# Reordered loads, a copy on GpSimd and a shifted transpose in the first slots of a forgetting-attention kernel

## The chip, the cores and the metric

The kernel runs on one core of a Trainium2 chip. The metric is the device time of one launch in microseconds (us); lower is better. The engines are named as the profile names them: PE is TensorE, DVE is VectorE, ACT is ScalarE, POOL is GpSimd, SP is SyncE.

## The reference, cut to what matters

Eight batches of eight heads, 576 tokens, head size 64. Attention with a forget gate `f`, then a two-layer network on the rows of all heads.

```python
scores = scale * q @ k.T                       # 8 x 8 x 576 x 576
cum = cumsum(log(clip(f, 1e-4, 1)))            # along the tokens
scores = where(causal, -1e9, scores + cum[i] - cum[j])
attn = softmax(scores) ;  x = (attn @ v) as rows of 512
h = x @ w_in ;  out = (h - tanh(h)) @ w_out    # 4608 x 512 -> 2048 -> 512
```

## The kernel before

The attention is worked in 32 slots, one for each pair of neighbouring heads (`pairs`, four pairs to a batch); slot p is pair p. The first four slots (batch 0) fill the machine: all that follows mixes attention with the network's products.

**A slot** has seven score tiles (`TILES`), numbered ti 0 to 6: three of the first head, one short "tail" tile (ti 3, `LAST`) with the last 64 tokens of both heads, three of the second head. `scores` (L337) multiplies a tile on PE into a PSUM bank, and ACT takes the exponential (L361) into a tile `e`; the tail tile goes to one of three kept tiles `EL[0..2]`, by pair number modulo 3. The banks are two of the pool `ps_sc` in turn, and in batch 0 every third tile uses the bank `ps_tr`; a bank is free for PE again once its exponential has been taken.

**Operands.** q and k of a pair are loaded with a cast by POOL's DMA queue (`load_qk`), turned by PE transposes into PSUM, and copied out by two copies to QT and KT (`trans`, L287): "VV" puts both on DVE, "AV" the first on ACT. With a string in the tuple ("VA", "Vv"), only the first copy is issued at once; the second goes into a list `LATER`, which `rest()` empties. Each head's rows 64 to 66 of QT and KT hold the decay: the running sum `cum` is split into `chi` and `clo` (L189, L190). For head 0 of batch 0 three rows of KT are copied by DVE (L191); the other heads' rows come by small DMAs (`aug_rows`, `bulk`).

**Values.** `values` (L382) multiplies e by v one slot later, 15 matmuls for each head, at ti 2 and ti 4 of the next slot in batch 0. DVE divides (L398 to L400), and `turn` (L407) transposes the result into XR, which the network reads. In slot 4 the first network products appear: `mlp1` (L451) with the first half of `win`, whose contraction has four parts, one for each pair; the first three parts are issued ahead of the last.

**The order** of every engine's instructions is the program's, written by hand: `start`, `bulk`, and then `att_items(p)` for each slot. For each ti the items stand in the order scores, loads of the table `LOADS`, transposes, values, turns. POOL's queue in order at the start: q and k of heads 0 to 3 (L149 to L152), the tail values `load_v_rest` (L123), the values of heads 0 and 1 (L127), the mask `late` (L169), then `bulk`: a small DMA of chi rows into QT (L212), q and k of heads 4 to 7, the values of heads 2 to 7 in four blocks (L131). Then come the `LOADS`: q and k of batch 1's heads 0 to 3, the first half of `win` (L222), q of batch 1's heads 4 to 7, and in slot 1 at ti 3 the function `last` (L585): four POOL memsets, of KT[1]'s margin, of two parts of vn[1], and of `EL[2]` (L589), which is the tail tile of slot 2. `unread` issues matmuls whose results nobody reads.

Of the kernel before, what the change touches and what calls it, by code (L numbers as in the profile page):

```python
# [21 lines left out]
def kernel(  # L22
# [10 lines left out]
    nc = tc.nc  # L33
    P = 128

    B, H, S, D = q.shape
    NH = B * H
# [3 lines left out]
    NPAIR = H // 2  # L41
# [28 lines left out]
    def m_bank(name):  # L70
        while M_AT[0] % 3 in KEPT:
            M_AT[0] += 1
        M_AT[0] += 1
        return ps_m.tile([P, 512], FP32, tag=f"m{(M_AT[0] - 1) % 3}", name=name)
# [18 lines left out]
    qn, kn = ([t[0:S // NT6, :].rearrange("p (h n d) -> p h n d", h=H, n=NT6) for t in raw] for raw in (qraw, kraw))  # L93
    qb, kb = ([t[:, 0:NJ * DM].rearrange("p (n e) -> p n e", n=NJ) for t in raw] for raw in (qraw, kraw))
    vn = [qkp.tile([P, NJ, H, VW], FP16, tag=f"vn{i}", name=f"vn{i}") for i in range(2)]
    QT = [qkp.tile([D + 3, H, S], FP16, tag=f"QT{i}", name=f"QT{i}") for i in range(2)]
    KT = [qkp.tile([D + 3, H, PITCH], FP16, tag=f"KT{i}", name=f"KT{i}") for i in range(2)]
# [3 lines left out]
    def load_qk(dst, src, b, h0, h1):  # L101
        nc.gpsimd.dma_start(
            out=dst[b % 2][:, h0:h1, :, :].rearrange("p h n d -> p h (n d)"),
            in_=src[b, h0:h1, :, :].rearrange("h (p n) d -> p h (n d)", n=NT6))
# [17 lines left out]
    def load_v_rest(b):  # L122
        nc.gpsimd.dma_start(out=vn[b % 2][0:S % P, NJ - 1, :, 0:D],  # L123
                            in_=v[b, :, S - S % P:S, :].rearrange("h p d -> p h d"))

    def load_v_head(b, h):
        nc.gpsimd.dma_start(out=vn[b % 2][:, 0:NJ - 1, h, 0:D],  # L127
                            in_=v[b, h, 0:S - S % P, :].rearrange("(n p) d -> p n d", p=P))

    def load_v_block(b, n, h0, h1):  # L130
        nc.gpsimd.dma_start(out=vn[b % 2][:, n, h0:h1, 0:D],  # L131
                            in_=v[b, h0:h1, n * P:(n + 1) * P, :].rearrange("h p d -> p h d"))
# [3 lines left out]
    NX = NH + 3  # L136
# [23 lines left out]
    chi = cst.tile([NX, S], FP16)  # L160
    clo = cst.tile([NX, S], FP16)
# [1 line left out]
    nc.vector.memset(vn[0][D:P, NJ - 1, :, :], 0.0)  # L163
    mul_k, add_k, mul_l, mul_q, add_q, both = (per[:, i:i + 1] for i in range(6))
    EL = [cst.tile([P, 192], FP16, tag=f"el{i}", name=f"el{i}") for i in range(3)]
    load_v_rest(0)
    load_v_head(0, 0)
    load_v_head(0, 1)
    nc.gpsimd.affine_select(out=late, in_=late, compare_op=ALU.is_ge, fill=-60000.0,  # L169
                            base=0, pattern=[[1, P]], channel_multiplier=-1)  # L170

# [16 lines left out]
                                 op0=ALU.mult, op1=ALU.add)  # L188
    nc.vector.tensor_scalar(out=chi, in0=cum, scalar1=mul_k, scalar2=add_k, op0=ALU.mult, op1=ALU.add)  # L189
    nc.vector.scalar_tensor_tensor(out=clo, in0=cum, scalar=mul_l, in1=chi, op0=ALU.mult, op1=ALU.subtract)  # L190
    nc.vector.tensor_copy(out=KT[0][NH:NX, 0, 0:S], in_=clo[NH:NX, :])  # L191

    def aug_rows(b):
        i, h0 = b % 2, 0 if b else 1
        hs = slice(b * H + h0, (b + 1) * H)
        return [(KT[i][D:D + 1, h0:H, 0:S], chi[hs, :]), (KT[i][D + 1:D + 2, h0:H, 0:S], clo[hs, :]), (QT[i][D + 2:D + 3, h0:H, :], chi[hs, :])]

    def load_aug(b):
        for to, of in aug_rows(b):
            nc.sync.dma_start(out=to, in_=of)  # L200
# [6 lines left out]
    const_rows(0)  # L207

    def bulk():
        (k_hi, chi_0), (k_lo, clo_0), (q_hi, _) = aug_rows(0)  # L210
        nc.sync.dma_start(out=k_hi, in_=chi_0)
        nc.gpsimd.dma_start(out=q_hi, in_=chi_0)  # L212
        nc.sync.dma_start(out=k_lo, in_=clo_0)
        load_qk(qn, q, 0, 4, 6)
        load_qk(kn, k, 0, 4, 6)
        load_qk(qn, q, 0, 6, H)
        load_qk(kn, k, 0, 6, H)
        for n in range(NJ - 1):
            load_v_block(0, n, 2, H)
# [67 lines left out]
    def trans(b, c, src, dst, early, copies, split=False):  # L287
        pn, g3 = S // NT6, NT6 // 2
        if early:
            t32 = m_bank("t32")  # L290
        elif KEPT and src is kn:
            t32 = ps_m.tile([P, UW], FP32, tag=f"m{KEPT[0]}", name="t32")
        else:
            t32 = ps_tr.tile([P, UW], FP32, tag="tr", name="t32")
        t16 = t32.bitcast(FP16)[:, 0:2 * S // 2].rearrange("p (a g n) -> p a g n", a=2, g=g3)
        for a in range(2):
            for g in range(g3):
                nc.tensor.transpose(out=t16[:, a, g, :],  # L298
                                    in_=src[b % 2][:, 2 * c + a, 2 * g:2 * g + 2, :],
                                    identity=id16[0:pn, 0:pn])  # L300
        parts = [(a, e) for a in range(2) for e in range(2)] if split else [(slice(0, 2), e) for e in range(2)]

        def copy(a, e, eng):
            if split:
                a = slice(a, a + 1)
            to = dst[b % 2][0:D, 2 * c:2 * c + 2, e:S:2].rearrange("d a (p g) -> d a p g", g=g3)[:, a]
            of = t16[e * D:(e + 1) * D, :, :, :].rearrange("d a g p -> d a p g")[:, a]
            if eng == "A":
                nc.scalar.activation(out=to, in_=of, func=AF.Copy)
            else:  # L310
                nc.vector.tensor_copy(out=to, in_=of)  # L311

        todo = [lambda a=a, e=e, eng=eng: copy(a, e, eng) for (a, e), eng in zip(parts, copies)]
        now = 1 if copies in ("VA", "Vv") else 2
        for fn in todo[:now]:
            fn()
        if now == 1:
            LATER.extend(todo[now:])
        return todo[now:]
# [54 lines left out]
    AV = {}  # L374
# [193 lines left out]
    pairs = [(b, c) for b in range(B) for c in range(NPAIR)]  # L568
# [22 lines left out]
    def att_items(p):  # L591
        def put(fn, *args):
            items.append((lambda: fn(*args), True))

        items = []
        here = pairs[p] if p < len(pairs) else None
        before = pairs[p - 1] if 0 < p <= len(pairs) else None
        after = pairs[p + 1] if p + 1 < len(pairs) else None
        early = p < NPAIR
        for ti in range(len(TILES)):  # L600
            if here and (p > 0 or ti > 1):
                put(scores, *here, ti)
            if p == 1 and ti == 6:
                items.append((lambda: const_rows(1), False))
                items.append((lambda: load_aug(1), False))
            if p == 0 and ti in (2, 5, 6):
                put(unread, {2: 6, 5: 4, 6: 2}[ti])
            if p == 1 and ti == 3:
                put(last)
            for load in LOADS.get((p, ti), ()):  # L610
                items.append((load, False))
            at_q, at_k = (1, 2) if p == 0 else (None, 0) if early else (0, 2) if p == NPAIR else (0, 3)
            if ti == 5 and p < NPAIR - 1:
                put(trans, *pairs[p + 2], qn, QT, True, "VV")
            if p in (2 * NPAIR - 1, 2 * NPAIR, 2 * NPAIR + 1) and (ti % 2 or ti == 0):
                items.append((rest, False))
            if p in (2 * NPAIR - 1, 2 * NPAIR) and ti % 2 == 0:
                pair = pairs[2 * NPAIR + 2 * (p - 2 * NPAIR + 1) + ti // 4]
                put(trans, *pair, *((kn, KT) if ti % 4 else (qn, QT)), False, "VA")
            if ti == at_q and p < 2 * NPAIR - 1:  # L620
                put(trans, *after, qn, QT, early, "VV")
            if p == NPAIR:
                if ti in (4, 5):
                    put(mlp1, 0, ti - 4, 1)
                    items.append((rest, False))
            if ti == at_k and p < 2 * NPAIR - 1 and p != NPAIR:
                put(trans, *after, kn, KT, early, "AV" if p in (0, 2) else "VV")
            if p == NPAIR:
                if ti == 0:
                    put(turn, *pairs[1])  # L630
                elif ti == 1:
                    put(turn, *pairs[p - 2])
                    put(values, *before)
                    put(mlp1, 0, 0, 0)
                elif ti == 2:
                    put(mlp1, 0, 1, 0)
                    put(turn, *before, True)
                    put(trans, *after, kn, KT, early, "Vv")
            elif early and ti in (2, 4) and before:
                put(values, *before, (ti // 2 - 1,))  # L640
            elif not early and ti == 2 and before:
                put(values, *before, (0, 1), p == NPAIR + 2)
            if p < NPAIR:
                if ti == 1 and p == 2:
                    put(turn, *pairs[0], True)
            elif p > NPAIR and ti == 3:
                items.append((release, False))
                put(turn, *before)
        return items
# [8 lines left out]
    for p in range(len(pairs) + 1):  # L658
        b, c = divmod(p, NPAIR)
        items = att_items(p)  # L660
# [53 lines left out]
```

## Time and profile before

| what | value |
|---|---|
| median of 3 runs | 338.80 us (338.78 to 339.18) |
| the profiled execution's own time | 338.77 us |
| its span in the trace | 337.1 us |
| PE, DVE, ACT, POOL busy | 330.0, 260.8, 233.2, 163.2 us |
| granted TensorE clock | 1.00 of full |

The span is the time from the first to the last instruction of the trace; the rest of the execution's time, 1.67 us, lies around it. A row of a timeline gives start, duration, engine, line, operation, tiles, and in brackets how long the engine stood idle before it and who released it. A duration of several merged instructions ("x4") reaches from the first start to the last end. ACT's and DVE's instructions overlap by some tenths of a us at their ends, so the pitch of a row is from start to start. "DMA ... us" in the list of DMA issues is the time from the issue's start to landing.

### The profile page before, as it was taken

What the parts mean: (1) busy time and instruction counts of PE and PEld (TensorE: products, weight loads), DVE (VectorE), ACT (ScalarE), POOL (GpSimd) and SP (SyncE); (2) the same over time, 40 slices, a digit from 0 to 9 for tenths busy, and PEclk for the clock granted to TensorE, in tenths of its full rate; (3) what the DMA queues carried; (4) which work ended last, traced back from release to release, by engine and by line L of the source; (5) the groups of instructions that cost most, each with busy time, mean ns of one, the idle gap of its engine ahead of it and who ended that gap; (6) DMA issues with size and microseconds to landing.
All of it is one profiled execution on the core that took longest, in us unless ns stands there. A gap on an engine that the chain in (4) does not pass through costs nothing.

```text
span 337.1 us, 8726 instructions
## 1 busy us (share of the span) xinstructions
PE 330.0 (98%) x3313; PEld 235.6 (70%) x3313; DVE 260.8 (77%) x509; ACT 233.2 (69%) x438; POOL 163.2 (48%) x321
## 2 busy tenths in 40 slices
PE   8899999999999999999999999999999999999996
PEld 8775558875687558845888888656865686486485
DVE  7998986659887886778867896788668866966865
ACT  6997777978977886788677867787558733632630
POOL 8977467775667564767377637722322210000000
PEclk9999999999999999999999999999999999999999
DMA  9999999999979997999899999990130022002003
GB/s 113 143 203 202 186 198 165 184 159 172 142 87 190 136 134 72 164 152 139 94 122 187 118 112 117 163 132 18 51 113 2 19 65 97 2 31 95 0 12 116
DMA packets 147468, 38.82 MB, mean 115 GB/s; under 512 B 128181, under 2 KB 146335, under 8 KB 147426
## 3 DMA queue, kind: packets, MB, share of 16 engines
q0 software_dynamic: 94528, 18.37, 75.5%
q1 hardware_dynamic: 52892, 19.89, 32.4%
q8 instruction: 26, 0.43, 0.6%
q14 instruction: 16, 0.13, 0.2%
q10 hardware_dynamic: 6, 0.01, 0.0%
HBM read 36.85 MB, written 9.44 MB: 137 GB/s over the span
## 4 chain that ended last, share of the span: by engine, by line
PE 90%; DVE 7%; ACT 2%; issue 1%; ACTq 0%
PE hps L451 36%; PE ops L517 29%; PE ps L352 11%; PE av L389 8%; PE ops L492 4%; DVE KT L311 2%; DVE QT L311 1%; PE t L298 1%; ACT e L361 1%; DVE xn L400 1%; DVE gq L462 0%; DVE TQ L187 0%; ACT th L456 0%; PE x L417 0%; DVE clo L190 0%
## 5 line engine op out<-in xcount | busy, mean ns | idle before, releaser
L451 PE MATMUL hps<-XR,win 128*128 128x512 f16 (+1 forms) x640 | 140.7, 357 | 0.3 <-DVE gq L462 0.3
L456 ACT ACTIVATE th<-hps 128x512 f32<-128x512 f32 x144 | 86.6, 602 | 55.5 <-PE hps L451 53.5
L361 ACT ACTIVATE e<-ps 128x512 f16<-128x512 f32 x192 | 110.2, 597 | 8.9 <-PE ps L352 7.4
L462 DVE TENSOR_TENSOR gq<-hps,th 128x512 f16<-128x512 f32 x144 | 98.0, 687 | 23.6 <-ACT th L456 22.0
L371 POOL TENSOR_SCALAR_AFFINE_SELECT e<-e 128x128 f16<-128x128 f16 x168 | 60.7, 364 | 71.5 <-ACT e L361 68.7
L451 PEld LDWEIGHTS <-win 128*128 128x128 f16 x640 | 57.7, 97 | 49.0 <-issue 1.1
L352 PE MATMUL ps<-QT,KT 67*128 67x64 f16 (+4 forms) x384 | 76.5, 276 | 2.0 <-DVE KT L311 1.4
L517 PEld LDWEIGHTS <-gq 128*128 128x128 f16 x640 | 60.3, 97 | 11.1
L517 PE MATMUL ops<-wout,gq 128*128 128x256 f16 x512 | 63.2, 272 | 0.0
L352 PEld LDWEIGHTS <-KT 67*128 67x128 f16 x384 | 36.4, 98 | 23.4 <-DVE KT L311 2.0
L389 PEld LDWEIGHTS <-e 128*128 128x128 f16 x896 | 32.3, 97 | 3.6
L389 PE MATMUL av<-vn,e 128*128 128x65 f16 x896 | 33.6, 193 | 0.0
L517 PE MATMUL ops<-W,sq 128*128 128x256 f16 x256 | 31.2, 272 | 0.0
L131 POOL DMA_DIRECT2D vn<-in_v_dram x32 | 28.0, 877 | 6.5 <-DMA win<-in_moe_w_in_dram 2.9
L400 DVE TENSOR_TENSOR xn<-av,rs 128x640 f16<-128x640 f32 x32 | 26.4, 825 | 1.3 <-DVE rs L399 0.2
L517 PEld LDWEIGHTS <-sq 128*128 128x128 f16 x256 | 24.1, 97 | 3.4
L108 POOL DMA_DIRECT2D kn<-in_k_dram x25 | 21.2, 848 | 2.1 <-issue 1.8
L108 POOL DMA_DIRECT2D qn<-in_q_dram x25 | 21.2, 848 | 1.8 <-issue 1.4
L371 POOL TENSOR_SCALAR_AFFINE_SELECT el<-el 128x128 f16<-128x128 f16 x28 | 9.3, 333 | 26.1 <-ACT el L361 25.8
L398 DVE TENSOR_SCALAR rs<-av 128x10 f32<-128x10 f32 x32 | 5.2, 163 | 18.2 <-PE av L389 17.0
L532 ACT ACTIVATE m<-ops 128x512 f32<-128x512 f32 x16 | 9.5, 596 | 10.9 <-PE ops L517 10.9
L484 DVE TENSOR_TENSOR gq<-gq 128x512 f16<-128x512 f16 x32 | 17.1, 533 | 0.0
(83 smaller groups left out, 311.8 us busy)
## 6 DMA issues: line engine op xcount, KB each, us to landing
out_dram<-ost SPq DMA_DIRECT2D x34, 256.0 KB
vn<-in_v_dram POOLq DMA_DIRECT2D x24, 128.0 KB, 6.2
qn<-in_q_dram POOLq DMA_DIRECT2D x20, 128.0 KB, 5.0
kn<-in_k_dram POOLq DMA_DIRECT2D x20, 128.0 KB, 5.6
win<-in_moe_w_in_dram POOLq DMA_DIRECT2D x2, 1024.0 KB, 11.8
wout<-in_moe_w_out_dram POOLq DMA_DIRECT2D x2, 1024.0 KB, 15.6
XR<-xn SPq DMA_TRANSPOSE x56
qn<-in_q_dram POOLq DMA_DIRECT2D x6, 144.0 KB, 4.6
```

The costliest lines, as they stand in the source:

```text
L108: nc.gpsimd.dma_start(out=dst[b % 2][0:pn, n, :].rearrange("p (h d) -> p h d", h=H), in_=src[b, :, n * P:n * P + pn, :].rearrange("h p d - ...
L131: nc.gpsimd.dma_start(out=vn[b % 2][:, n, h0:h1, 0:D], in_=v[b, h0:h1, n * P:(n + 1) * P, :].rearrange("h p d -> p h d"))
L352: nc.tensor.matmul(out=ps[:, col:col + n], lhsT=kt[0:rows, h, j * P:(j + 1) * P], rhs=qt[0:rows, h, i0:i0 + n], start=True, stop=cut == 0)
L361: nc.scalar.activation(out=e[:, lo:hi], in_=ps[:, lo:hi], func=AF.Exp, bias=-SHIFT, scale=qscale)
L371: nc.gpsimd.affine_select(out=view, in_=view, compare_op=ALU.is_ge, fill=0.0, base=0, pattern=pat, channel_multiplier=-1)
L389: nc.tensor.matmul(out=av[:, a, ib, :], lhsT=E.pop((b, c, a, j, ib)), rhs=vn[b % 2][:, j, 2 * c + a, 0:D + 1], start=(j == 0), stop=(j == ib))
L400: nc.vector.tensor_tensor(out=xn.rearrange("p i (a d) -> p a i d", a=2), in0=av[:, :, :, 0:D], in1=rs.to_broadcast([P, 2, NJ, D]), op=ALU. ...
L451: nc.tensor.matmul(out=hps[:, o:o + n], lhsT=win[:, ci, ft * P:(ft + 1) * P], rhs=XR[:, ci, t:t + n], start=(ci == 0), stop=(ci == NCH - 1))
L456: nc.scalar.activation(out=th, in_=hps, func=AF.Tanh, scale=-1.0)
L462: nc.vector.tensor_tensor(out=GQ[(u, i)][:, half, kt, :], in0=hps, in1=th, op=ALU.add)
L484: nc.vector.tensor_tensor(out=LHS[name](u, i)[:, ks], in0=LHS[x](u, i)[:, ks], in1=LHS[y](u, i)[:, ks], op=op)
L517: nc.tensor.matmul(out=ps[:, m, :], lhsT=LHS[lhs](u, kt // 4)[:, kt % 4, m * P:(m + 1) * P], rhs=rhs[:, kt, :], start=(fresh and (apart or ...
```

## The change

The changes are all in the start and in slots 0 and 2. In POOL's queue, q of heads 4 and 5 is loaded where the tail values and head 1's values were, and these two go behind k of heads 4 and 5 in `bulk`. The chi rows for QT are sent from the place ahead of `bulk`, and the three clo rows of head 0 are copied to KT by POOL, behind that DMA, where DVE did it. The transposes of q's heads 4 and 5 move from ti 5 of slot 0 to its tail tile, ti 3, with both copies still on DVE, the second kept back one place. The second copy of k's heads 2 and 3 (ti 2, "Av" now where it was "AV") is kept back with it, so that DVE's order is: first copy of q 4/5, second copy of k 2/3, second copy of q 4/5. In slot 2 the value product of the pair before's first head is issued at ti 3 where it was ti 2.

```diff
-    load_v_rest(0)
+    load_qk(qn, q, 0, 4, 6)
     load_v_head(0, 0)
-    load_v_head(0, 1)
...
-    nc.vector.tensor_copy(out=KT[0][NH:NX, 0, 0:S], in_=clo[NH:NX, :])
+    nc.gpsimd.dma_start(out=QT[0][D + 2:D + 3, 1:H, :], in_=chi[1:H, :])
+    nc.gpsimd.tensor_copy(out=KT[0][NH:NX, 0, 0:S], in_=clo[NH:NX, :])
...
     def bulk():
-        (k_hi, chi_0), (k_lo, clo_0), (q_hi, _) = aug_rows(0)
+        (k_hi, chi_0), (k_lo, clo_0), _ = aug_rows(0)
         nc.sync.dma_start(out=k_hi, in_=chi_0)
-        nc.gpsimd.dma_start(out=q_hi, in_=chi_0)
         nc.sync.dma_start(out=k_lo, in_=clo_0)
-        load_qk(qn, q, 0, 4, 6)
         load_qk(kn, k, 0, 4, 6)
+        load_v_rest(0)
+        load_v_head(0, 1)
         load_qk(qn, q, 0, 6, H)
...
-        now = 1 if copies in ("VA", "Vv") else 2
+        now = 1 if copies in ("VA", "Vv", "Av") else 2
...
-            if ti == 5 and p < NPAIR - 1:
+            if ti == 5 and 0 < p < NPAIR - 1:
                 put(trans, *pairs[p + 2], qn, QT, True, "VV")
...
-                put(trans, *after, kn, KT, early, "AV" if p in (0, 2) else "VV")
+                put(trans, *after, kn, KT, early, "Av" if p == 0 else "AV" if p == 2 else "VV")
+            if p == 0 and ti == 3:
+                put(trans, *pairs[2], qn, QT, True, "Vv")
+                items.append((rest, False))
...
-            elif early and ti in (2, 4) and before:
-                put(values, *before, (ti // 2 - 1,))
+            elif early and ti in (3 if p == 2 else 2, 4) and before:
+                put(values, *before, (ti // 4,))
```

## The prediction

> **What bounds the kernel now.** I read the page's chain first, then the busy time by stretch, then the timelines of each engine up to 34 us.
>
> ```profile
> span 337.1 us, 8726 instructions
> ...
> PE 90%; DVE 7%; ACT 2%; issue 1%; ACTq 0%
> ```
>
> ```profile
> 16.84:20.96 4.12, 3.82 (x72) 3.19 (x70) 4.01 (x8) 3.98 (x9) 4.00 (x9) 1.00 1.25 199
> 33.40:42.00 8.60, 8.60 (x81) 4.85 (x81) 7.98 (x14) 6.36 (x13) 4.13 (x10) 1.00 1.71 185
> ```
>
> The chain is PE's in nine tenths, and from 33.4 us on PE has no idle time (8.60 of 8.60 us): there only work counts, and the change alters no work of PE. What it can win or lose is the moment at which the filling stage, up to about 29 us, hands over to PE. In slot 2 (16.84 to 20.96; the columns are its length, then PE, PEld, DVE, ACT, POOL busy) DVE and ACT are full within 0.15 us and PE has 0.3 us free: three engines are near their limit together, so a gain of one is soon stopped by another. POOL is full as well, with 4.00 of 4.12 us. That column is the one to watch, since the change gives POOL more to do ahead of it.
>
> The profiled execution took 338.77 us, 1.67 around its span of 337.1, against a median of 338.80; I make the sum against 338.8.
>
> **The start: DVE's copy goes to POOL.**
>
> ```profile
> 6.91 0.81 DVE L190 SCALAR_TENSOR_TENSOR clo<-TQ,per,chi 67x576 f16<-67x576 f32 x1
> 7.76 0.30 DVE L191 COPY KT<-clo 3x576 f16<-3x576 f16 x1
> 8.09 1.97 DVE L311 COPY KT<-t 64x288 f16<-64x288 f16 x4
> 10.26 1.62 DVE L311 COPY QT<-t 64x576 f16<-64x576 f16 x2 [0.20 <-PE t L298]
> 12.22 0.81 DVE L311 COPY KT<-t 64x576 f16<-64x576 f16 x1 [0.34 <-ACT KT L309]
> ```
>
> ```profile
> 19.36 0.38 PE L352 MATMUL ps<-QT,KT 67*128 67x512 f16 x1 [0.30 <-ACT e L361]
> ```
>
> Without L191 the four copies of KT start at 7.76, 0.33 us earlier. PE's first scores need the first two of them (half of 1.97 us) and L191's rows, so they start 0.33 earlier too, if POOL's copy is there by 7.76 + 0.98 = 8.74. The second stall, 0.34 us at 12.22 where DVE waits for ACT's copy, is filled by the first copy of q 4/5 (0.81 us); that makes the second copy of k 2/3 end near 13.2, which was 13.0 (12.22 + 0.81). PE's first tile of slot 1 waits for that, so PE and ACT keep about 0.2 us of gain through slot 1. DVE alone could keep 0.33 + 0.34 = 0.67 us, but in slot 2 its division waits for a product behind the PE tile at 19.36, and that waits for ACT. So the gain to carry is 0.2 us, up to 0.67 if ACT and PE let DVE through.
>
> **POOL's queue, instruction by instruction.**
>
> ```profile
> 4.29 0.71 POOL L123 DMA_DIRECT2D vn<-in_v_dram  x1
> 4.97 1.54 POOL L127 DMA_DIRECT2D vn<-in_v_dram  x2
> 6.48 0.55 POOL L169 TENSOR_SCALAR_AFFINE_SELECT late<-late 128x128 f16<-128x128 f16 x1
> 7.17 0.54 POOL L212 DMA_DIRECT2D QT<-chi  x1
> 7.70 0.68 POOL L102 DMA_DIRECT2D qn<-in_q_dram  x1
> 8.37 0.64 POOL L102 DMA_DIRECT2D kn<-in_k_dram  x1
> ...
> 10.24 3.32 POOL L131 DMA_DIRECT2D vn<-in_v_dram  x4
> ...
> 16.05 0.83 POOL L222 DMA_DIRECT2D win<-in_moe_w_in_dram  x1
> ```
>
> ```profile
> 18.15 0.53 POOL L587 MEMSET vn<- 64x528 f16 x1
> 18.74 0.18 POOL L588 MEMSET vn<- 128x80 f16 x1
> 18.84 0.26 POOL L589 MEMSET el<- 128x192 f16 x1
> ```
>
> Before, all is issued back to back from 7.17 to 19.1. After: q 4/5 (0.68) and head 0's values (0.76) take 4.29 to 5.73, `late` ends near 6.3, and then POOL waits for chi, which ends just before clo starts (6.91). The chi DMA runs to 7.47, and POOL waits for clo (6.91 + 0.81 = 7.72). The copy starts at 7.77. Its price is in no row: DVE needs 0.30 us for it (L191); POOL's own rows are
>
> ```profile
> 30.26 0.31 POOL L371 TENSOR_SCALAR_AFFINE_SELECT e<-e 128x128 f16<-128x128 f16 x1
> ...
> 38.13 0.43 POOL L371 TENSOR_SCALAR_AFFINE_SELECT e<-e 128x256 f16<-128x256 f16 x1
> ```
>
> that is 0.12 us for 128 more columns, so 0.31 + 3.5 x 0.12 = 0.73 us for 576 columns read and written; a memset of 528 columns, which reads nothing, takes 0.53. I take 0.70, near the select, which reads and writes as the copy does; ends 0.30 and 1.1 (twice the memset). The copy ends at 8.47, ahead of DVE's 8.74, so the start's gain holds. The Trainium skill, "GPSIMD Engine Reference", section 3.1, gives about 769 ns for 512 elements at best in a loop of its cores; scaled to 576, an estimate of 0.87 us, with which POOL's queue and the result would be 0.17 us later. No row here shows it; the selects' slope speaks for less.
>
> k 4/5 then goes out at 8.50, where it was 8.37: +0.13. Behind it come the tail values (4.29 to 4.97: 0.68) and head 1's values (half of 4.97 to 6.48: 0.76). So everything from q 6/7 on is **0.13 + 0.68 + 0.76 = 1.57 us later**, through a queue that has no gap up to 19.1. The four issues of v's blocks move from 10.24 to 11.8; the memset of EL[2] ends at 19.10 + 1.57 = **20.67**.
>
> **What waits for that memset.** EL[2] is the tail tile of slot 2: its exponential writes columns that the memset has to have cleared first.
>
> ```profile
> 19.68 0.28 ACT L361 ACTIVATE el<-ps 128x128 f16<-128x128 f32 x1
> 19.89 3.40 ACT L361 ACTIVATE e<-ps 128x512 f16<-128x512 f32 x6
> ...
> 22.19 1.09 ACT L361 ACTIVATE e<-ps 128x512 f16<-128x512 f32 x2
> ```
>
> Before, the memset was done 0.58 us ahead of it. After, ACT is there at 19.5 and stands until 20.71: **1.03 us later than before**, and the 0.2 of gain is swallowed. Behind it in ACT's order stand all exponentials of slots 2 and 3; behind those, for their banks, PE's tiles from ti 6 of slot 2 on. Some comes back: two exponentials of 0.6 take 1.09, a pitch of 0.49, while the six from 19.89 took 3.40, a pitch of 0.56, for they waited now and then for PE. Walking the banks through slots 2 and 3 (PE starts a tile 0.05 after its bank's exponential ends; the exponential can start about 0.5 later), ACT's copies to XR end at 28.0.
>
> ```profile
> 26.77 0.66 ACT L421 ACTIVATE XR<-x 128x576 f16<-128x576 f16 x1
> ```
>
> ```profile
> 27.28 0.81 PE L451 MATMUL hps<-XR,win 128*128 128x512 f16 x3
> ...
> 28.94 0.45 PE L417 MATMUL x<-id,xn 128*128 128x128 f16 x5
> ```
>
> They ended at 27.43 (26.77 + 0.66): so 0.57 of the 1.03 is left. The first network product's third part needs that copy; it began about 27.71 (two pitches of 0.216 behind 27.28) and will begin at 28.04: +0.33. From there PE runs to the turn at 28.94, which before stood 0.1 us for DVE's division
>
> ```profile
> 28.05 0.82 DVE L400 TENSOR_TENSOR xn<-av,rs 128x640 f16<-128x640 f32 x1
> ```
>
> (done at 28.87). That leaves 0.23 to 0.33 us at the turn, and the rest follows one for one: **+0.3 us, 339.1**. If ACT won back none of the 0.46, it would be +0.75; with a copy of 0.30 us POOL is 0.4 earlier and the sum about -0.1; with one of 1.1 it is +0.7.
>
> **The other edits.** The value product a tile later costs PE nothing: at ti 3 it stands ahead of the tile at 19.36, where PE waited for ACT. The cover is needed, for
>
> ```profile
> vn<-in_v_dram POOLq DMA_DIRECT2D x1, 96.0 KB, 4.9
> ...
> win<-in_moe_w_in_dram POOLq DMA_DIRECT2D x1, 1024.0 KB, 10.1
> ```
>
> the last block (the fourth of the issues at L131, begun at 12.73, landing 4.9 later, at 17.6) lands by 19.2 at the worst, ahead of the time when ACT moves again. If the tail did not stall, it could cost PE up to 0.4. The first half of win (issue 16.05, landing 26.15) moves by 1.57 at most, to 27.7; PE wants it at 27.55. Transfers behind one another hide part of a late issue, so I put it at 27.0 and at nothing. The transposes of q 4/5 take PE the same time at ti 3 as at ti 5.
>
> **The rivals.**
> 1. The tail doesn't decide, ACT keeps the start's gain: -0.2, 338.6. For it: POOL's spans are rough, and a queue with fewer transfers behind one another may issue faster. Against: 0.58 us of slack, 1.57 of delay.
> 2. DVE sets the hand-over alone, and both its savings arrive: -0.67, 338.1. For it: the division at 28.05 and its turn are DVE's. Against: ACT's and PE's full columns.
> 3. Slower: POOL's copy is the decisive price. From 0.97 us on (8.74 less 7.77) it also holds the first scores; at 1.1 to 1.3 the memset ends at 21.1 to 21.3, and the sum is +0.7 to +0.9: 339.6. The skill's 0.87 would be half way there.
> 4. win lands late: POOL's delay stays whole and the transfers queue as well, landing at 28.2 where 27.55 is wanted; +0.6 beyond the forecast's 0.3, of which the wait for XR hides 0.1: 339.6.
>
> **How the numbers follow.** A measurement can tell about 0.2%, 0.68 us, so faster begins at 338.1 and slower at 339.5. Forecast 0.45, of which 0.06 is over 339.5; rival 1 0.15 (0.02 faster); rival 2 0.12 (0.10 faster); rival 3 0.15 (0.11 slower); rival 4 0.13 (0.11 slower). Faster 0.12, slower 0.28, same 0.60. The range goes from rival 2's time to somewhat over rivals 3 and 4: 338.1 to 339.9.
>
> **What would show it.** In the changed trace the row of L191 stands on POOL, with 0.6 to 0.8 us; PE's first scores start near 8.8; the memset of EL[2] ends at 20.5 to 20.9 and the tail exponential of slot 2 starts right behind it, with ACT idle for about a us; the turn that was at 28.94 stands near 29.2. I am wrong if the memset ends before 20.0, if ACT has no gap there, if DVE rather than ACT holds the turn, or if PE waits for win at the first product.

## The result and the profile after

The changed kernel takes **339.94 us** (median of 22 runs, 339.16 to 342.18) where the kernel before takes 338.81 (338.77 to 339.18): a ratio of 1.0042, interval 1.0029 to 1.0054. It is slower by 1.13 us, and its runs are spread over 3 us where those of before lie within 0.4. The profiled execution took 339.62 us with a span of 337.9, so it lies below the median: 0.8 us of the loss is in it.

First POOL's timeline (start, length, instruction; the bracket is the idle time ahead of it and what ended it):

```profile
5.70 0.66 POOL L168 TENSOR_SCALAR_AFFINE_SELECT late<-late 128x128 f16<-128x128 f16 x1
7.17 0.54 POOL L190 DMA_DIRECT2D QT<-chi  x1 [0.82 <-DVE chi L188]
7.89 0.66 POOL L191 COPY KT<-clo 3x576 f16<-3x576 f16 x1 [0.18 <-DVE clo L189]
8.50 0.67 POOL L102 DMA_DIRECT2D kn<-in_k_dram  x1
...
17.65 0.85 POOL L222 DMA_DIRECT2D win<-in_moe_w_in_dram  x1
...
20.48 0.26 POOL L589 MEMSET el<- 128x192 f16 x1
```

The copy stands on POOL with 0.66 us, and POOL stands idle for 0.82 us ahead of the chi rows, for the start of its queue is too short now. From q of heads 6 and 7 on all of POOL's work is 1.6 us later: that load is issued at 10.61 (before 9.00), win at 17.65 (before 16.05), and EL[2] is cleared by 20.74 (before 19.10).

ACT's timeline shows who waits for that memset, and how much is left of it at the copies to XR:

```profile
20.78 0.28 ACT L361 ACTIVATE el<-ps 128x128 f16<-128x128 f32 x1 [1.16 <-POOL el L589]
20.95 3.04 ACT L361 ACTIVATE e<-ps 128x512 f16<-128x512 f32 x6
...
27.44 0.66 ACT L421 ACTIVATE XR<-x 128x576 f16<-128x576 f16 x1
```

Then PE's timeline at the start, in slot 2 and where the first network products begin:

```profile
8.84 0.38 PE L352 MATMUL ps<-QT,KT 67*128 67x512 f16 x1
...
20.99 0.43 PE L298 MATMUL t<-id,qn 96*128 96x96 f16 x6 [0.63 <-DMA qn<-in_q_dram]
...
26.44 0.44 PE L417 MATMUL x<-id,xn 128*128 128x128 f16 x5
...
27.59 0.19 PE L389 MATMUL av<-vn,el 128*128 128x65 f16 x1
28.27 0.82 PE L451 MATMUL hps<-XR,win 128*128 128x512 f16 x3 [0.49 <-DMA win<-in_moe_w_in_dram]
...
29.80 0.44 PE L417 MATMUL x<-id,xn 128*128 128x128 f16 x5
```

The 0.49 us ahead of the first product (L451) are new: before, PE went from the last value product straight into it. The DMA view of the issues around 17.65 has the load it waits for (size, then us from issue to landing), and the page's chain has it too:

```profile
win<-in_moe_w_in_dram POOLq DMA_DIRECT2D x1, 1024.0 KB, 10.6
```

```profile
PE 89%; DMA 3%; POOL 3%; DVE 2%; ACT 1%; issue 0%; ACTq 0%; POOLq 0%
PE hps L451 36%; PE ops L517 29%; PE ps L352 11%; PE av L389 8%; PE ops L492 4%; DMA win<-in_moe_w_in_dram 3%; PE t L298 1%; POOL vn L131 1%; ACT e L361 1%; POOL kn L102 1%; POOL qn L102 1%; DVE gq L462 0%; DVE TQ L186 0%; ACT th L456 0%; DVE clo L189 0%
```

The chain that ended last was PE, DVE and ACT alone. Now it goes from PE's product to win's transfer (3% of 337.9 us, that is its 10.6) and from there back through POOL's issues, value block by value block, to clo on DVE. That is one whole path the kernel before did not have: the copy of clo, POOL's queue, the transfer of win.

Followed along PE's order (start of the same instruction in both traces, in us):

| instruction | before | after | difference |
|---|---|---|---|
| first scores | 9.12 | 8.84 | -0.28 |
| first turn, slot 2 | 17.68 | 17.48 | -0.20 |
| turn of pair 1 | 25.26 | 25.93 | +0.67 |
| next turn | 26.09 | 26.44 | +0.35 |
| first product | 27.28 | 28.27 | +0.99 |
| turn that was at 28.94 | 28.94 | 29.80 | +0.86 |
| end | 337.1 | 337.9 | +0.8 |

So the start's gain came and was kept through slot 1, the tail tile took it away and 0.35 more, the wait for win made 0.99 of it, and 0.86 goes through to the end. The 0.63 us that PE waits for q of batch 1 at 20.99 is no further loss. In a second profile of the same kernel (below) that wait is missing, PE waits 0.34 us for ACT's tail tile at the next tile instead, and the two turns stand at the same 25.93 and 26.44.

### The profile page after: what moved, and what is told of

It reads as the page before. It is cut to its first block, busy times and chain, and to the rows that moved or that the text cites. A ratio compares the mean times of both kernels' runs of the same rounds, so it can differ in the third digit from the quotient of the medians.

```text
span 337.9 us, 8728 instructions
## 1 busy us (share of the span) xinstructions
PE 330.9 (98%) x3313; PEld 236.9 (70%) x3313; DVE 260.8 (77%) x508; ACT 232.9 (69%) x438; POOL 163.4 (48%) x322
## 4 chain that ended last, share of the span: by engine, by line
PE 89%; DMA 3%; POOL 3%; DVE 2%; ACT 1%; issue 0%; ACTq 0%; POOLq 0%
PE hps L451 36%; PE ops L517 29%; PE ps L352 11%; PE av L389 8%; PE ops L492 4%; DMA win<-in_moe_w_in_dram 3%; PE t L298 1%; POOL vn L131 1%; ACT e L361 1%; POOL kn L102 1%; POOL qn L102 1%; DVE gq L462 0%; DVE TQ L186 0%; ACT th L456 0%; DVE clo L189 0%
## 5 line engine op out<-in xcount | busy, mean ns | idle before, releaser
L451 PE MATMUL hps<-XR,win 128*128 128x512 f16 (+1 forms) x640 | 140.7, 357 | 0.8 <-DMA win<-in_moe_w_in_dram 0.5
L371 POOL TENSOR_SCALAR_AFFINE_SELECT e<-e 128x128 f16<-128x128 f16 x168 | 60.0, 361 | 69.6 <-ACT e L361 67.6
L451 PEld LDWEIGHTS <-win 128*128 128x128 f16 x640 | 57.7, 97 | 49.6 <-issue 1.1
L371 POOL TENSOR_SCALAR_AFFINE_SELECT el<-el 128x128 f16<-128x128 f16 x28 | 9.5, 340 | 26.4 <-ACT el L361 26.3
L532 ACT ACTIVATE m<-ops 128x512 f32<-128x512 f32 x16 | 9.5, 596 | 10.9 <-PE ops L517 10.9
```

The costliest lines, as they stand in the source:

```text
L371: nc.gpsimd.affine_select(out=view, in_=view, compare_op=ALU.is_ge, fill=0.0, base=0, pattern=pat, channel_multiplier=-1)
L451: nc.tensor.matmul(out=hps[:, o:o + n], lhsT=win[:, ci, ft * P:(ft + 1) * P], rhs=XR[:, ci, t:t + n], start=(ci == 0), stop=(ci == NCH - 1))
```

## The experiments

Two theories, named WIN and TAIL where the expectations name them. **WIN**: what costs is that win's first half lands after PE is ready for it; the stalls ahead of it are hidden in that wait. **TAIL**: what costs is ACT's stall at EL[2], as predicted, only dearer. None of the kernels leaves out work; two of them add memsets of a tile that nobody reads. The medians of the kernel before beside these runs were 338.80 to 338.88.

### The stall taken out, and each delay made alone

**e1**: the change, with EL[2] cleared in POOL's wait for chi.

```diff
     nc.gpsimd.affine_select(out=late, in_=late, compare_op=ALU.is_ge, fill=-60000.0,
                             base=0, pattern=[[1, P]], channel_multiplier=-1)
+    nc.gpsimd.memset(EL[2], 0.0)
...
-        nc.gpsimd.memset(EL[2], 0.0)
```

> The change with the memset of EL[2] moved ahead, into POOL's wait for chi near 6.4 us, so that the tail exponential of slot 2 waits for nothing. Theory TAIL (the memset's delay makes the loss): the stall of 1.16 us on ACT goes and the time falls to 338.6, 0.2 below before. Theory WIN (the late landing of win's first half makes it): ACT runs ahead but PE still waits for win at the first product until about 28 us, so the time stays at 339.6 to 339.9.

Measured: 339.69 us (339.32 to 340.52), ratio 1.0027 (1.0018 to 1.0036). PE's waits of its first 34 us:

```profile
PE hps L452 <- DMA win<-in_moe_w_in_dram: 0.7, 1, 0.7
```

Without the stall three quarters of the loss is still there, and the wait for win is 0.7 us here where it was 0.5: PE came earlier and stood longer. TAIL is not the main loss.

**e8** and **e9**: the kernel before, with three memsets of a 128 x 512 scratch tile on POOL (1.76 us, near the change's delay), once ahead of win's load with EL[2] cleared early by DVE, once behind win and ahead of EL[2]'s memset.

```diff
-    for e in EL[0:2]:
+    for e in EL:
...
-             (1, 0): [lambda: load_win(0, DFF // 2)],
+             (1, 0): [lambda: nc.gpsimd.memset(scratch, 0.0)] * 3 + [lambda: load_win(0, DFF // 2)],
...
-        nc.gpsimd.memset(EL[2], 0.0)
```

> The kernel before with three memsets of a scratch tile on POOL ahead of win's first load (about 1.6 us) and EL[2] cleared by DVE at the start: win late and the tail not, nothing else changed. WIN: win lands at 27.7 to 28.2 where 27.3 is wanted, 339.2 to 339.8, with the spread of the change. TAIL: 338.8.

Measured: 340.15 us (339.14 to 340.94), ratio 1.0034 (1.0024 to 1.0044). Its DMA view, PE's wait at the product and ACT's tail tile:

```profile
win<-in_moe_w_in_dram POOLq DMA_DIRECT2D x1, 1024.0 KB, 10.4
```

```profile
28.53 0.82 PE L452 MATMUL hps<-XR,win 128*128 128x512 f16 x3 [0.72 <-DMA win<-in_moe_w_in_dram]
```

```profile
20.02 0.29 ACT L362 ACTIVATE el<-ps 128x128 f16<-128x128 f32 x1
```

The tail tile is on time, and of the change only the lateness of win and of what stands behind it on POOL is in this kernel; e9, where all but one of these later loads are late too, costs 0.2 us. Its start is 0.35 us later as well (DVE clears one tile more), and that lasts to the turn ahead of the product (26.45 for 26.09). So of the 1.28 us by which it is slower than the kernel before beside it, some 0.35 are the start's, and the late load gives about 0.9. That is most of the change's loss, and a spread of 1.8 us comes with it.

```diff
     def last():
+        for _ in range(3):
+            nc.gpsimd.memset(scratch, 0.0)
```

> The kernel before with the same three memsets ahead of the four memsets of slot 1: the tail is late by 1.6 us and win's first load is not. It prices the tail's stall alone. By the prediction's walk through the banks +0.3, 339.1; 339.5 if ACT wins nothing back; 338.8 if all of it is hidden.

Measured: 339.06 us (339.02 to 339.42), ratio 1.0005 (0.9997 to 1.0014). ACT's tail tile and the product behind it:

```profile
20.74 0.28 ACT L362 ACTIVATE el<-ps 128x128 f16<-128x128 f32 x1 [0.94 <-POOL el L592]
```

```profile
27.58 0.91 PE L452 MATMUL hps<-XR,win 128*128 128x512 f16 x3
```

The stall that I had predicted, alone: 0.94 us of wait on ACT, 0.30 us at PE's product, about 0.2 us of time (its interval includes no change), and no more spread than before. That is what TAIL is worth.

### The parts of the change alone

**e2** has only the new order of the loads, **e3** only the chi rows' earlier place and the copy on POOL, **e4** only the transposes of q 4/5 at the tail tile with their copies.

```diff
-    load_v_rest(0)
+    load_qk(qn, q, 0, 4, 6)
     load_v_head(0, 0)
-    load_v_head(0, 1)
...
-        load_qk(qn, q, 0, 4, 6)
         load_qk(kn, k, 0, 4, 6)
+        load_v_rest(0)
+        load_v_head(0, 1)
```

> The kernel before with the new order of loads alone: q 4/5 first, tail values and head 1's values behind k 4/5; the copy stays on DVE, the transposes at ti 5. POOL is 1.44 us later from q 6/7 on. TAIL: memset ends near 20.5, +0.2 to +0.4 at the turn, 339.1. WIN: win lands 1.5 to 2 later than 26.1, PE waits for it, 339.5 to 340.

```diff
-    nc.vector.tensor_copy(out=KT[0][NH:NX, 0, 0:S], in_=clo[NH:NX, :])
+    nc.gpsimd.dma_start(out=QT[0][D + 2:D + 3, 1:H, :], in_=chi[1:H, :])
+    nc.gpsimd.tensor_copy(out=KT[0][NH:NX, 0, 0:S], in_=clo[NH:NX, :])
...
-        nc.gpsimd.dma_start(out=q_hi, in_=chi_0)
```

> The kernel before with the chi DMA and the copy of clo's rows on POOL alone. POOL is 0.75 us later from q 4/5 on; DVE and PE start 0.33 earlier. Both theories: memset near 19.85, win at 26.9 to 27.2, just in time: 338.6 to 338.9. Below 338.6 if the start's gain comes through whole.

```diff
-        now = 1 if copies in ("VA", "Vv") else 2
+        now = 1 if copies in ("VA", "Vv", "Av") else 2
...
-            if ti == 5 and p < NPAIR - 1:
+            if ti == 5 and 0 < p < NPAIR - 1:
...
-                put(trans, *after, kn, KT, early, "AV" if p in (0, 2) else "VV")
+                put(trans, *after, kn, KT, early, "Av" if p == 0 else "AV" if p == 2 else "VV")
+            if p == 0 and ti == 3:
+                put(trans, *pairs[2], qn, QT, True, "Vv")
+                items.append((rest, False))
```

> The kernel before with q 4/5 turned at ti 3 of slot 0 alone, POOL's queue as before. DVE's 0.34 us of waiting are filled, the second copy of k 2/3 is up to 0.2 later. Both theories: POOL and win as before, so no loss: 338.6 to 338.9. If it is over 339.1, the new DVE order costs by itself.

Measured: e2 339.06 us (338.78 to 341.23), ratio 1.0016 (1.0003 to 1.0030); e3 339.00 (338.50 to 339.89), 1.0007 (0.9999 to 1.0016); e4 339.00 (338.89 to 339.43, and one of 344.43 at a granted clock of 0.984), 1.0004 (0.9996 to 1.0013). Only e2's interval is clear of no change, and barely. The parts come to 0.6 us, the whole to 1.13: they do not seem to add. The landings of win show why. e2 and e3 each delay POOL's queue by about half (0.85 and 0.77 us). For e2 the expectation had 1.44, which leaves out that q 4/5 no longer stands in the queue behind. So its time of 339.06, though it is near TAIL's figure, tests neither theory: ACT waits only 0.16 us at the tail tile there.

```profile
16.90 0.85 POOL L222 DMA_DIRECT2D win<-in_moe_w_in_dram  x1
```

```profile
16.82 0.84 POOL L222 DMA_DIRECT2D win<-in_moe_w_in_dram  x1
```

and PE's first product in the one, then in the other:

```profile
27.35 0.82 PE L451 MATMUL hps<-XR,win 128*128 128x512 f16 x3
```

```profile
27.61 0.82 PE L451 MATMUL hps<-XR,win 128*128 128x512 f16 x3 [0.43 <-DMA win<-in_moe_w_in_dram]
```

Before, win landed at 26.15 and was wanted at 27.28: 1.1 us of slack. A delay of 0.8 us alone eats most of it: e2's lands at 27.3, just in time; e3's lands at 27.5, after a transfer of 10.7 us, and its PE is 0.3 us early, so it waits. Both delays together go 0.5 past it. **Two delays spent the same slack.**

### Attempts to bring win in earlier

**e5**: the change, with win's first half loaded in two pieces, so that the first product needs only 256 of its columns. **e6**: e5 with e1's early memset.

```diff
-             (1, 0): [lambda: load_win(0, DFF // 2)],
+             (1, 0): [lambda: load_win(0, 2 * P), lambda: load_win(2 * P, DFF // 2)],
```

> The change with the first half of win loaded in two: the 256 columns that the first two products read, then the rest (one issue more on POOL). WIN: the first product no longer waits, the small piece lands near 24; the tail's stall stays (and is 0.8 longer, since the memset follows the extra issue): 339.2 to 339.5, with a small spread. TAIL: as the change or slower, 339.7 to 340.2.

> The change with both: the memset of EL[2] in POOL's wait for chi, and win's first 256 columns loaded apart. If these two waits are all that the change brought, the start's gain is left: 338.5 to 338.6, and the spread is as small as before's. If something else is lost, it stays over 338.8.

e5: **340.54 us** (339.83 to 343.78), ratio 1.0066 (1.0038 to 1.0095): no faster than the change, although PE no longer waits for win. The second issue stands ahead of the memset in POOL's queue. ACT's tail tile, the PE tile behind it, and the busy time by stretch (length, PE, PEld, DVE, ACT, POOL, then the granted clock):

```profile
21.52 0.28 ACT L361 ACTIVATE el<-ps 128x128 f16<-128x128 f32 x1 [1.75 <-POOL el L589]
```

```profile
21.85 0.30 PE L352 MATMUL ps<-QT,KT 67*128 67x320 f16 x1 [1.09 <-ACT el L361]
```

```profile
16.00:20.96 4.96, 4.45 (x81) 3.64 (x78) 4.57 (x10) 3.58 (x7) 4.86 (x8) 1.00 1.45 154
20.96:24.70 3.74, 2.84 (x34) 2.30 (x34) 3.64 (x5) 3.18 (x7) 3.68 (x8) 0.83 1.25 190
24.70:28.90 4.20, 3.79 (x50) 2.92 (x48) 1.78 (x5) 2.77 (x7) 2.01 (x3) 0.75 1.24 205
28.90:34.00 5.10, 5.08 (x66) 3.13 (x64) 3.86 (x8) 3.77 (x9) 3.11 (x5) 1.00 1.50 200
```

ACT stands for 1.75 us instead of 1.16, PE for 1.09, and the granted clock averages 0.83 and 0.75 over the next two stretches; in the trace it is 0.50 from 23.4 to 26.8 us and 1.00 on either side. In this execution the turn that was at 28.94 is 2.6 us later. The runs of e5 fall in three groups: six at 339.8 to 340.0, three at 341.1 to 341.4, three near 343.8, with a granted clock, over the whole span, of 1.0 (0.998 once), 0.995 and 0.985: the spread of this kernel is the clock's. The profile is of the middle group. The six runs at full clock are as slow as the change (339.94): the longer stall at the tail seems to cost what the wait for win did. One of the 35 runs of the kernel before beside e5, e6, e8 and e9 took 340.08, so a late execution, though rare, is not the change's alone.

e6: 340.10 us (339.01 to 341.58), ratio 1.0041 (1.0025 to 1.0057), though neither the stall nor the wait for win should be left. Both profiles that I have of it are of its fastest executions (339.03 and, taken once more, 339.09):

> The kernel with both waits taken away, a second look: its executions lie between 339.0 and 341.6 and the profile was of the fastest. If a transfer still decides, PE waits for v's blocks or batch 1's first q (18 to 21 us) in a slow execution; if none does, PE's clock or its start is late.

They show neither wait. The second shows the next transfers in the queue instead, in PE's waits:

```profile
PE av L391 <- DMA vn<-in_v_dram: 0.8, 1, 0.8
...
PE t L300 <- DMA kn<-in_k_dram: 0.4, 1, 0.4
```

So win is only the last of several loads that POOL's delay makes late: the values of slot 2 and q and k of batch 1 are at or past their due time too. What a typical execution of e6 loses stays open.

To see how much one kernel varies, the change was profiled once more, unchanged:

> The changed kernel itself, a second look, since its executions lie between 339.2 and 342.2 and one profile shows one of them. If win is the moving part, this profile's wait for win at the first product differs from 0.66 us at the same rate as its time from 339.6; if another transfer moves, that wait shows instead.

It took 340.25 us. The issue of win is at the same 17.65, the tail stalls the same, and the turns ahead of the product stand within 0.01 us of the first profile's; the transfer took longer, and the whole difference of 0.6 us is made at the product:

```profile
win<-in_moe_w_in_dram POOLq DMA_DIRECT2D x1, 1024.0 KB, 11.2
```

```profile
28.87 0.82 PE L451 MATMUL hps<-XR,win 128*128 128x512 f16 x3 [1.09 <-DMA win<-in_moe_w_in_dram]
```

That is one source of the spread, and the one that these two profiles show: a landing that varies by a microsecond costs nothing while there is 1.1 us of slack, and all of it when there is none. It accounts for the 0.6 us between these two, not for the runs up to 342. The change's runs of 342.03 and 342.18 have a granted clock of 0.995, all others one of 0.998 to 1.0, and e12 below shows a third source.

### The delay taken away

**e7**: the change, with head 1's values issued ahead of `late` and the memset of EL[2] behind it, which shortens POOL's delay to about 0.8 us. **e10**: e7, and k of batch 1's heads 2 and 3 issued behind win.

```diff
+    load_v_head(0, 1)
     nc.gpsimd.affine_select(out=late, in_=late, compare_op=ALU.is_ge, fill=-60000.0,
                             base=0, pattern=[[1, P]], channel_multiplier=-1)
+    nc.gpsimd.memset(EL[2], 0.0)
...
-        load_v_head(0, 1)
...
-        nc.gpsimd.memset(EL[2], 0.0)
```

> The change with head 1's values issued in POOL's wait for chi (they cost nothing there) and EL[2] cleared there too: POOL's delay falls from 1.6 to about 0.85 us. If the delay of POOL's queue is the cause, win lands near 27.2, about when PE wants it, the spread shrinks, and the time lies at 338.7 to 339.0. If the order of the transposes or of the values costs, it stays over 339.3.

> As the gap-filled kernel, and k of batch 1's heads 2 and 3 (wanted only near 29 us) issued behind win's first load: win is issued 0.65 us earlier and lands at 26.3 to 26.6, as in the kernel before. If late transfers are the whole loss, the start's gain of 0.2 to 0.3 is left: 338.5 to 338.7, faster than both. If it stays at 338.8 or over, the gain at the start is itself lost on the way.

Measured: e7 339.06 us (338.62 to 340.31), ratio 1.0012 (1.0003 to 1.0021); e10 339.01 (338.59 to 341.00), 1.0012 (0.9997 to 1.0026). Most of the loss is gone, but the gain at the start doesn't arrive: in e7's profile the chi rows took 4.6 us from issue to landing where the change's took 3.2, and PE's tail tile of slot 0 waits for them. One more load stands ahead of them in the queue; that this is why is not shown, for e10, with the same queue ahead of them, has 3.8.

```profile
11.82 0.19 PE L353 MATMUL ps<-QT,KT 67*128 67x64 f16 x1 [0.68 <-DMA QT<-chi]
```

**e11**: every part of the change, but POOL's queue kept at its times of before: the values that the change puts behind k 4/5 are issued while POOL would wait for chi and clo, and SP sends the chi rows.

```diff
+    load_v_rest(0)
+    load_v_head(0, 1)
...
-    nc.gpsimd.dma_start(out=QT[0][D + 2:D + 3, 1:H, :], in_=chi[1:H, :])
     nc.gpsimd.tensor_copy(out=KT[0][NH:NX, 0, 0:S], in_=clo[NH:NX, :])
...
         nc.sync.dma_start(out=k_lo, in_=clo_0)
+        nc.sync.dma_start(out=q_hi, in_=chi_0)
...
-        load_v_rest(0)
-        load_v_head(0, 1)
```

> The change, with GpSimd's queue kept at its old times: the remaining value blocks of head 0 and head 1's first values are issued while GpSimd would wait for the mask input anyway, and SyncE sends the decay rows into QT, so that the loads behind (q 6/7, batch 1, v blocks, the gate weights) are issued within 0.2 us of before. Theory WIN (the loss is the gate weights landing late because GpSimd's queue runs 1.6 us later): the 0.5 to 0.6 us wait of TensorE at the first gate product goes, the early start of 0.2 to 0.35 us is kept to the end, 338.5 to 338.7 us, and the spread is that of the kernel before (0.4 us or less). Theory TAIL (the late clearing of EL[2] is the loss): that clearing also comes at its old time, so 338.5 to 338.8 too. Theory PLACE (the new order of the values itself costs, head 0's and head 1's blocks landing ahead of k 4/5 and all that follows): TensorE waits in slot 0's tail or slot 1 for kn or vn, 339.0 to 339.5. If the start gain is eaten by TensorE's own filler running cold, 338.8 to 338.9.

Measured: **338.89 us** (338.62 to 339.29), ratio 1.0000 (0.9992 to 1.0009). POOL's issue of win, its transfer, and PE at the first product:

```profile
16.23 0.83 POOL L222 DMA_DIRECT2D win<-in_moe_w_in_dram  x1
```

```profile
win<-in_moe_w_in_dram POOLq DMA_DIRECT2D x1, 1024.0 KB, 10.3
```

```profile
8.76 0.38 PE L352 MATMUL ps<-QT,KT 67*128 67x512 f16 x1 [0.28 <-POOL KT L192]
...
11.59 0.19 PE L352 MATMUL ps<-QT,KT 67*128 67x64 f16 x1 [0.45 <-DVE QT L311]
...
27.60 0.81 PE L451 MATMUL hps<-XR,win 128*128 128x512 f16 x3
```

With POOL's delay down to 0.18 us the loss is gone whole, most of the spread with it (0.7 us), and win lands 1.1 us ahead of its use again (26.5 against 27.60). So the delay was the cause: made without the rest of the change (e8) it gives most of the loss, and the rest of the change without it (e11) costs nothing. The start is 0.36 us early here as well, and gives it back at 11.59, in slot 0's tail tile. The row names DVE's copy, but in e12 the same tile began at 11.16 while that copy ran until 11.50; what is later in e11 is the chi rows' DMA, the third in SP's queue. That is argued from the comparison, and no run separates it.

**e12**: the change, with the value product of slot 2 back at ti 2.

```diff
-            elif early and ti in (3 if p == 2 else 2, 4) and before:
-                put(values, *before, (ti // 4,))
+            elif early and ti in (2, 4) and before:
+                put(values, *before, (ti // 2 - 1,))
```

> The change with one part undone: the value product of slot 2 comes back to its old tile, behind the second tile rather than the third. Theory WIN: nothing, 339.7 to 340.2 as the change itself, since TensorE waits for the gate weights behind it either way. If the later value product was what the late v blocks need: TensorE waits 0.2 to 0.8 us for vn in slot 2 and the time is 340.0 to 340.6. If the moved product itself cost time: 339.2 to 339.5.

Measured: 339.70 us (339.02 to 342.22), ratio 1.0032 (1.0017 to 1.0047), within the change's own interval. PE in slot 2, at the first product and, this profile being of an execution of 341.68 us, later on:

```profile
18.88 0.31 PE L389 MATMUL av<-vn,e 128*128 128x65 f16 x5 [0.29 <-DMA vn<-in_v_dram]
...
28.39 0.82 PE L451 MATMUL hps<-XR,win 128*128 128x512 f16 x3 [0.61 <-DMA win<-in_moe_w_in_dram]
```

```profile
74.37 0.38 PE L451 MATMUL hps<-XR,win 128*128 128x512 f16 x1 [0.36 <-DMA XR<-xn]
...
107.74 1.03 PE L517 MATMUL ops<-wout,gq 128*128 128x256 f16 x8 [1.35 <-DVE ost L536]
```

The value product at its old place does wait for the last block, 0.29 us, and the waits behind it hide that (the turns stand at 25.93 and 26.43, as in the change): as far as these runs can tell, putting it a tile later neither costs nor brings anything. The lower rows are another source of the spread. This execution lost 0.98 us by the turn at 28.94, as the change does, and some 1.9 us more behind it, at a DMA transpose and behind DVE, which itself waited 1.8 us for the transposed k. In e10's profile DVE waited 2.0 us for the transposed k and PE 0.7 us behind it. Why those transfers come late in some executions stays open; no run of e11 took longer than 339.29 us.

## Why the prediction was wrong

I had forecast 339.1, range 338.1 to 339.9. It is 339.94: slower, where "same" had the larger chance, and just outside the range. Point by point:

- **The start** (0.33 expected, 0.2 kept): 0.28 at the first scores and 0.20 at slot 2. Right. In other executions with the same start it was 0.36 at the first scores (e11, and the change once more).
- **POOL's copy** (0.70 us, ends 0.30 and 1.1): 0.66. The rows of the selects gave it better than the Trainium skill's "GPSIMD Engine Reference", section 3.1, whose figure came to an estimate of 0.87.
- **POOL's queue** (1.57 us later): 1.60 at win, 1.64 at the end of EL[2]'s memset (20.74 for 20.67). Right.
- **The tail** (ACT stands to 20.71, XR's copy ends at 28.0, +0.3 us): ACT's tile starts at 20.78, the copy ends at 28.10, and e9 measures the step by itself as +0.30 at the product, +0.25 at the turn and about +0.2 us of time. Right, mechanism and size.
- **The value product**: costs nothing, as said (e12).
- **The first half of win: this is the step that failed.** I wrote that it "moves by 1.57 at most, to 27.7; PE wants it at 27.55", and then "I put it at 27.0 and at nothing", because transfers behind one another would hide part of a late issue. It landed at 28.25: 17.65 and 10.6. From issue to landing it took not 0.7 us less, as 27.0 needed, but 0.5 more. Before, the product stood 1.19 us behind the turn at 26.09; behind the turn at 26.44 PE was so ready about 27.63, and it began at 28.27: 0.64 us lost, of which 0.13 came back at the turn's wait for DVE. The last sign that I had named for being wrong, PE waiting for win at the first product, is there. This was my fourth rival, with 28.2, 0.6 us and 339.6, at a chance of 0.13. It gives the profiled execution's 339.62; the median lies 0.3 higher, between that execution and the second one, whose wait for win was 1.09 us.

The landings of the runs side by side show why the assumption did not hold (in the order of the issue; e5 and e6 load win in two pieces and are left out):

| kernel | issue | us to landing | landing | PE's first product |
|---|---|---|---|---|
| e4 | 16.01 | 11.0 | 27.0 | 27.40, no wait |
| e9 | 16.02 | 9.7 | 25.7 | 27.58, no wait |
| before | 16.05 | 10.1 | 26.15 | 27.28, no wait |
| e11 | 16.23 | 10.3 | 26.5 | 27.60, no wait |
| e10 | 16.29 | 10.9 | 27.2 | 27.23, no wait |
| e3 | 16.82 | 10.7 | 27.5 | 27.61, waits 0.43 |
| e2 | 16.90 | 10.4 | 27.3 | 27.35, no wait |
| e7 | 16.90 | 9.4 | 26.3 | 27.84, no wait |
| e1 | 17.64 | 10.2 | 27.8 | 27.93, waits 0.65 |
| e12 | 17.64 | 10.7 | 28.3 | 28.39, waits 0.61 |
| after | 17.65 | 10.6 | 28.25 | 28.27, waits 0.49 |
| after, once more | 17.65 | 11.2 | 28.85 | 28.87, waits 1.09 |
| e8 | 18.07 | 10.4 | 28.5 | 28.53, waits 0.72 |

The load takes 9.4 to 11.2 us, and a later issue does not shorten it: the five issued up to 16.29 average 10.4 us, the five from 17.64 on 10.6. So a later issue is, on average, a later landing, whole. My 27.0 needed 9.4, which one of the thirteen executions has. The row for the 10.1 was in my working, and so was the use; the honest sum, 17.62 + 10.1 = 27.72 against 27.55, already was past the due time, and it left nothing for the one to two microseconds by which the same transfer varies. I had the slack of the memset to a hundredth and priced the transfer with a hope.

A price taken without these rows would have been further off. The Trainium skill, "DMA: Bandwidth & Descriptors", section "Anatomy of one DMA — SWDGE (gpsimd) path", fits a load as 2.0 us and its bytes at 436 KB per us; for this 1 MB that is an estimate of 4.4 us. The rows here have 9.4 to 11.2, with the loads of batch 1 in the same queue ahead of it.

## What to carry to other kernels

Where a queue of loads is delayed, list every load behind the delay with its issue, its time to landing and its first use, each from its own row, and count the delay whole; a slack smaller than what that time varies by is no slack. Slack is spent once: two edits that each cost little alone can cost a microsecond together, as e2 and e3 do. And an engine that issues the loads pays for a small job twice, with the job and with its wait for the job's input. Here the copy cost its 0.66 us and 0.18 us of waiting for clo, and with two issues moved behind the copy POOL stood idle for 0.82 us ahead of the chi rows, until e11 put the issues back into that wait.

## What the runs showed of the hardware

- The same 1 MB load with a cast, from the same issue time, took 10.6 us in one execution and 11.2 in another; in e1 it took 10.2. Issued near 16.0 us it took 9.7 in e9, 10.1 in the kernel before and 11.0 in e4.
- In e5's profile the granted clock was 0.50 for 3.4 us, from 23.4 to 26.8, and the longest wait of PE ahead of it was 1.09 us, up to 21.85. A wait of that length does not decide it alone: six of e5's twelve runs had a clock of 0.998 to 1.0, and the change's second profile has a wait of 1.09 us at the first product and a clock of 1.00 behind it. What decides it stays open. The Trainium skill, "TensorE: Matmul & The Clock Gate", section "What's actually happening", has the clock fall after at least one idle window of some 3.4 us; no wait of that length is in these rows. Its section "A second HAM failure mode: psum-queue depth-cycling" tells of short idle times between groups of matmuls that do it too, and that is nearer to what e5 shows, though no run separates it.
- GpSimd copied 3 x 576 numbers of fp16 in 0.66 us, where VectorE took 0.30.
